# Moving two weight conversions from between the last token mixing products into the eighth and the last attention tile

## The chip, the cores and the metric

The kernel runs on one core of one Trainium2 chip. Its time is device microseconds from launch to end. TensorE (PE) multiplies, VectorE (DVE) and ScalarE (ACT) work on elements, GpSimd (POOL) takes some element work and the indirect transfers, SyncE (SP) issues nearly all other transfers.

## The reference, cut to what matters

Three blocks follow each other: an attention with a decaying state, a token and channel mixing block, and a mixture of experts whose expert is chosen token by token. All weights of the middle block are float64 in the input.

```python
def reference(r, k, v, w, u, moe_..., moe2_...):
    x = attention(r, k, v, w, u)            # 2 x 768 tokens x 384
    xt = x.transpose(0, 2, 1)
    h = np.maximum(xt @ w_tok1, 0.0) @ w_tok2      # token mixing, 768 -> 256 -> 768
    u = x + h.transpose(0, 2, 1)
    h2 = np.maximum(u @ w_ch1, 0.0) @ w_ch2        # channel mixing, 384 -> 1536 -> 384
    return moe2(u + h2, ...)                       # 8 experts, 384 -> 1024 -> 384
```

## The kernel before, in words

**Attention.** The 1536 tokens are 12 tiles of 128, and the loop `for t in range(NT)` makes one pass for each: passes 0 to 5 are the first batch, 6 to 11 the second. The instructions are written out by hand and every engine keeps its own order, so a late instruction holds back all that stand behind it on its engine. In pass t VectorE scales the inputs of tile t+2 (`pre_rk`, tile `rk`), masks the scores of tile t+1 (`masks`, two `am`), multiplies `pp` for tile t+2, and adds the output of tile t (`finish`, tile `x`). ScalarE then rounds `x` to `xh`, and GpSimd makes the remainder `xl` (L473); TensorE multiplies in pairs hi and lo.

**Conversions.** A float64 weight matrix arrives as pairs of 32-bit words in a buffer `raw` (two of them in turn, 768 KB each). There are 16 conversions, numbered 0 to 15, two halves for each of eight matrices: 0 and 1 for `t1`, 2 and 3 for `t2`, 4 and 5 for `c10`, 6 and 7 for `c20`, 8 and 9 for `c11`, 10 and 11 for `c21`, 12 and 13 for `c12`, 14 and 15 for `c22`. One conversion is

- ScalarE: an absolute value (L305, `conv_abs`);
- VectorE: two short operations (L314, L315) and two longer ones (L319, L321), in `conv_parts`; after the last one the load of the conversion two further on is issued (`conv_load`, L275);
- one step later (`conv_finish`): a rounding on ScalarE (L281) and a subtraction on GpSimd (L282) that gives the low part.

`CONV_T` lists the passes that hold conversions 0, 1, 2 and so on. `CONV_N` says how many of its steps stand ahead of `finish` in the pass. A pass without a conversion only finishes the one before it.

**Token mixing.** `mix1` runs in the passes and gathers into two accumulators. The second product (`mix2`) of the first batch has six parts: parts 1 to 5 stand in passes 7 to 11 and part 6 right behind the loop. All six use the same accumulator (`k=2`), and VectorE adds each part to `xT` (L515) before the next may start. In pass 10 `usplit(0)` lets VectorE make three `ul` tiles (L526) behind the addition of part 4.

**Behind the loop** stand `turn(11)`, the first two steps of channel mixing (`ch1` 0 and 1) with the last `mix1` between them, and the six parts of `mix2` for the second batch, which take three accumulators in turn. `conv_tail` puts conversions 8 and 9 between them, by `CONV_B` and `ABS_B`. From channel mixing's step 2 on, each step holds one more conversion, 10 to 15.

Of the kernel before, what the change touches and what calls it, by code (L numbers as in the profile page):

```python
# [28 lines left out]
W_LO, W_HI = 0.55, 1.25  # L29
WARM = (6, 12, 3)  # L30
T1 = 4
CONV_T = (2, 3, 4, 5, 6, 8, 9, 10)
CONV_B = (1, 1, 1, 1, 1, 1, 0, -1, 0, 0)
ABS_NEXT = (10, 11, 12, 13, 14)
ABS_B = (0, 3)
CONV_N = (0, 0, 0, 1, 1, 1, 1, 1, 1, 1, 1, 0)
HI_MIN, HI_MAX = (float(x) for x in np.array([0x38100000, 0x47EFFFFF], np.int32).view(np.float32))

# [33 lines left out]
@with_exitstack  # L72
def moe_chain_kernel(ctx, tc, a_in, wu, u_row, wt1, wt2, wc1, wc2, wgl, wex, cst_in, cst_a, out):
    with tc.manual_schedule():
        _emit(ctx, tc, a_in, wu, u_row, wt1, wt2, wc1, wc2, wgl, wex, cst_in, cst_a, out)


def _emit(ctx, tc, a_in, wu, u_row, wt1, wt2, wc1, wc2, wgl, wex, cst_in, cst_a, out):
# [55 lines left out]
    def load_a(t, part=None):  # L134
        if t not in a_t:
            rk = ap.tile([128, 1024], F32, tag="rk", name=f"rk{t}", bufs=4)
            v = ap.tile([128, DM], F32, tag="v", name=f"v{t}", bufs=3)
            a_t[t] = (rk, v)
        for p, (dst, c0) in enumerate(zip(a_t[t], (0, 1536))):
            if part is None or p == part:  # L140
                nc.sync.dma_start(out=dst, in_=a_in[t, :, c0:c0 + dst.shape[1]])
# [136 lines left out]
    def conv_finish():  # L278
        if conv_pend:
            f, hs, ls = conv_pend.pop()  # L280
            nc.scalar.copy(hs, f)  # L281
            nc.gpsimd.tensor_tensor(out=ls, in0=f, in1=hs.bitcast(F32), op=ALU.subtract)  # L282
# [4 lines left out]
    def conv_abs(n):  # L287
        k, h = conv[n]
        name = ("t1", "t2", "c10", "c20", "c11", "c21", "c12", "c22")[k]
        if h == 0:  # L290
            pool = wtp if k < 2 else wbl if k < 5 else wb2[0]
            W[name] = tuple(pool.tile([128, 1536], F32R, tag=f"b{2 * k + j}", name=name) for j in range(2))
        raw = conv_raw.pop(0)
        parts = tuple(x[:, h * 768:(h + 1) * 768] for x in W[name])
        if wb2:
            if n < 12:
                late[n % 2] = cpool_[0].tile([128, 1536], I32, tag=f"raw{6 + n % 2}", name="f")
            f, mag = late[n % 2][:, 0:768], late[n % 2][:, 768:1536].bitcast(F32)
        else:
            if n % 2:  # L300
                f = hp.tile([128, 768], I32, tag="row", name="f", bufs=1)
            else:
                f = ap.tile([128, 768], I32, tag="f", name="f", bufs=1)
            mag = f.bitcast(F32)
        nc.scalar.activation(out=mag, in_=raw[:, :, 1].bitcast(F32), func=ACTF.Abs)  # L305
        conv_mag[n] = raw, mag, f, parts

    def conv_parts():
# [16 lines left out]
                conv_abs(n + 1)  # L325
            yield
        conv_finish()

    tail_at = [-1]

    def conv_tail(n):
        tail_at[0] += 1
        for j in range(2):
            if ABS_B[j] == tail_at[0]:
                conv_abs(8 + j)
        if n < 0:
            conv_finish()
        else:
            conv_do(n)

    conv_work = conv_parts()

    def conv_do(n=3):
        for _ in range(n):
            next(conv_work, None)
# [68 lines left out]
    def values(t):  # L414
        b, c = divmod(t, NCH)
        rk, v = a_t[t]
        am = am_t.pop(t)
        y = ps_tile("y", (128, DM))
        for q in range(4):
            if c > 0:  # L420
                nc.tensor.matmul(y[:, q * 96:(q + 1) * 96], lhsT=rk[:, q * 128:(q + 1) * 128], rhs=sts[(t - 1) % 3][:, q], start=(q == 0), stop=False)
        for h in range(8):
            q, hh = divmod(h, 2)
            for g in range(2):
                r = slice(64 * g, 64 * g + 64)
                nc.tensor.matmul(y[r, h * D:(h + 1) * D], lhsT=am[hh][:, q, r], rhs=v[:, h * D:(h + 1) * D], start=(c == 0 and h == 0), stop=(h == 7))
        y_t[t] = y
# [27 lines left out]
    def state(t):  # L455
        kpv = kp_t[t]
        if t % NCH > 0:
            for q in range(4):
                nc.scalar.activation(out=sts[t % 3][:, q], in_=kpv[:, q], func=ACTF.Copy, scale=w128[:, q:q + 1])
            return  # L460
        for g in range(2):
            ps, cs = slice(64 * g, 64 * g + 64), slice(48 * g, 48 * g + 48)
            nc.vector.tensor_tensor(out=sts[t % 3][ps, :, cs], in0=kpv[ps, :, cs], in1=w128[ps].unsqueeze(2).to_broadcast([64, 4, 48]), op=ALU.mult)

    def finish(t):
        b, c = divmod(t, NCH)
        x = ap.tile([128, DM], F32, tag="x", name="x")
        nc.vector.tensor_tensor(out=x, in0=y_t.pop(t), in1=bon_t.pop(t).rearrange("p h e -> p (h e)"), op=ALU.add)
        nc.sync.dma_start(out=x, in_=yscr[t], cond=bad > 0, cond_hint=False)
        xh[t] = ap.tile([128, DM], F32R, tag=f"xh{c}", name=f"xh{t}", bufs=1)  # L470
        xl[t] = ap.tile([128, DM], F32R, tag=f"xl{c}", name=f"xl{t}", bufs=1)
        nc.scalar.copy(xh[t], x)
        nc.gpsimd.tensor_tensor(out=xl[t], in0=x, in1=xh[t].bitcast(F32), op=ALU.subtract)  # L473
        xx[t] = x

    def turn(t):
        b, c = divmod(t, NCH)
        if c == 0:
            xT[b] = xtp.tile([128, 3, S], F32, tag=f"xT{b}", name=f"xT{b}")
        x = xx.pop(t)  # L480
        tp = ps_tile("tp", (128, DM))
        for k in range(3):
            nc.tensor.transpose(tp[:, k * 128:(k + 1) * 128], x[:, k * 128:(k + 1) * 128], CA("ident"))
        nc.scalar.copy(xT[b][:, :, c * 128:(c + 1) * 128], tp.rearrange("p (k j) -> p k j", k=3))
# [6 lines left out]
    def mix1(t):  # L491
        b, c = divmod(t, NCH)
        w1h, w1l = W["t1"]
        if c == 0:
            mix_ps[b] = [acc_tile(m) for m in range(2)]
        for m in range(2):
            o = c * 256 + m * 128
            mm3(mix_ps[b][m], w1h[:, o:o + 128], w1l[:, o:o + 128], xh[t], xl[t], c == 0, c == NCH - 1)
        if c == NCH - 1:
            for m in range(2):  # L500
                hi = ap.tile([128, DM], F32R, tag=f"t1h{m}", name="t1h", bufs=1)
                lo = ap.tile([128, DM], F32R, tag=f"t1l{m}", name="t1l", bufs=1)
                relu_split(mix_ps[b][m], hi, lo)
                t1[m] = (hi, lo)

    def mix2(b, half, c, k=2):
        w2h, w2l = W["t2"]
        ps = acc_tile(k)
        for m in range(2):
            hi, lo = t1[m]  # L510
            o = m * S + half * 384
            cs = slice(c * 128, (c + 1) * 128)
            mm3(ps, hi[:, cs], lo[:, cs], w2h[:, o:o + 384], w2l[:, o:o + 384], m == 0, m == 1)
        u = xT[b][:, c, half * 384:(half + 1) * 384]
        nc.vector.tensor_tensor(out=u, in0=u, in1=ps, op=ALU.add)  # L515
# [37 lines left out]
    for t in range(NT):  # L553
# [16 lines left out]
        if grow:  # L570
            update(t + 1)
            state(t + 1)
        if t in CONV_T:
            conv_abs(CONV_T.index(t))
        values(t)
        if t + 1 < NT:
            pre_bonus2(t + 1)
        if t + 3 < NT:
            load_a(t + 3, 1)
        if t in CONV_T:  # L580
            conv_do(CONV_N[t])
        else:
            conv_finish()
        finish(t)
        if t in CONV_T:
            conv_do(3 - CONV_N[t])
# [73 lines left out]
    def chan_step(n, f, side, then):  # L660
        ps = ch1(f)
        if f >= 3:
            next(side, None)
        if f == 11:
            then()
        if f >= 3:
            next(side, None)
        h = hsplit(ps)
        push(lambda: ch2(n, f, h))
        if n == 3 and f == 11:  # L670
            unit_ready(0)
        work()

    def chan(n, side, then, start=0):
        for f in range(start, 12):
            chan_step(n, f, side, then)
        for _ in side:
            pass

    conv_tail(CONV_B[0])  # L680
    turn(11)
    chan_step(0, 0, nothing, None)
    conv_tail(CONV_B[1])
    mix1(11)
    conv_tail(CONV_B[2])
    chan_step(0, 1, nothing, None)
    conv_tail(CONV_B[3])
    for half in range(2):
        for c in range(3):
            mix2(1, half, c, (2, 0, 1)[c])  # L690
            conv_tail(CONV_B[4 + 3 * half + c])
    actx.close()

    wb2.append(ctx.enter_context(tc.tile_pool(name="wb2", bufs=1)))
# [657 lines left out]
```

## Time and profile before

| what | value |
|---|---|
| median of 3 runs | 432.24 us (431.27 to 433.52) |
| the profiled execution | 428.3 us, its span 426.8 us |
| TensorE busy | 407.2 us, 95% of the span |
| VectorE busy | 278.3 us, 65% |
| ScalarE busy | 192.7 us, 45% |
| GpSimd busy | 92.6 us, 22% |
| mean granted TensorE clock | 0.984 |

The span runs from the first to the last instruction; the profiled execution is one of the program, with the profiler on. Its time lies 3.9 us under the median, and the launch around the span takes 1.5 us of it.

### The profile page before, as it was taken

What the parts mean: (1) busy time and instruction counts of PE and PEld (TensorE: products, weight loads), DVE (VectorE), ACT (ScalarE), POOL (GpSimd) and SP (SyncE); (2) the same over time, 40 slices, a digit from 0 to 9 for tenths busy, and PEclk for the clock granted to TensorE, in tenths of its full rate; (3) what the DMA queues carried; (4) which work ended last, traced back from release to release, by engine and by line L of the source; (5) the groups of instructions that cost most, each with busy time, mean ns of one, the idle gap of its engine ahead of it and who ended that gap; (6) DMA issues with size and microseconds to landing.
All of it is one profiled execution on the core that took longest, in us unless ns stands there. A gap on an engine that the chain in (4) does not pass through costs nothing. (4 is left out here: it accounts for less than half of the span.)

```text
span 426.8 us, 8281 instructions
## 1 busy us (share of the span) xinstructions
PE 407.2 (95%) x3172; PEld 387.6 (91%) x3172; DVE 278.3 (65%) x590; ACT 192.7 (45%) x461; POOL 92.6 (22%) x83
## 2 busy tenths in 40 slices
PE   7999699998899799999999999999999999999994
PEld 4888598897798799999999999999999999999994
DVE  6859998788979944623362447568677677675431
ACT  2677468475443331213221221452755666655531
POOL 2014236236233310000000001131362132121110
PEclk9999999999999699999999999999999999999998
DMA  7544475132390000100100010871779866663000
GB/s 250 196 150 143 156 262 191 44 137 74 129 363 27 2 1 2 55 2 0 39 19 2 1 57 1 330 295 61 241 288 409 278 217 233 215 209 102 6 35 14
DMA packets 16799, 55.86 MB, mean 131 GB/s; under 512 B 3921, under 2 KB 7795, under 8 KB 16754
## 3 DMA queue, kind: packets, MB, share of 16 engines
q1 hardware_dynamic: 14834, 49.96, 33.3%
q0 software_dynamic: 1920, 5.32, 4.0%
q8 instruction: 26, 0.43, 0.4%
q14 instruction: 19, 0.16, 0.1%
HBM read 52.31 MB, written 5.91 MB: 136 GB/s over the span
## 5 line engine op out<-in xcount | busy, mean ns | idle before, releaser
L1014 DVE TENSOR_TENSOR we<-wr,we 128x768 fp32r<-128x768 f32 x54 | 51.6, 960 | 16.0 <-ACT we L1013 15.7
L353 ACT ACTIVATE hh<-c 128x384 fp32r<-128x384 f32 x48 | 23.5, 490 | 73.6 <-PE c L350 64.9
L354 DVE SCALAR_TENSOR_TENSOR hl<-c,hh 128x384 fp32r<-128x384 f32 x48 | 26.5, 553 | 42.9 <-ACT hh L353 42.9
L353 ACT ACTIVATE hh<-e 128x256 fp32r<-128x256 f32 (+1 forms) x72 | 25.2, 351 | 56.9 <-PE e L350 42.3
L348 PE MATMUL c<-uh,c 128*128 128x384 f32 x144 | 48.8, 339 | 2.1 <-ACT c L281 2.1
L348 PE MATMUL acc<-hh,c 128*128 128x384 f32 x144 | 50.2, 349 | 0.0
L354 DVE SCALAR_TENSOR_TENSOR hl<-e,hh 128x256 fp32r<-128x256 f32 (+1 forms) x72 | 27.2, 378 | 35.2 <-ACT hh L353 35.1
L349 PE MATMUL c<-uh,c 128*128 128x384 f32 x144 | 48.8, 339 | 1.2 <-POOL c L282 1.2
L349 PE MATMUL acc<-hh,c 128*128 128x384 f32 x144 | 48.8, 339 | 0.0
L350 PE MATMUL acc<-hl,c 128*128 128x384 f32 x144 | 48.8, 339 | 0.0
L350 PE MATMUL c<-ul,c 128*128 128x384 f32 x144 | 48.5, 337 | 0.0
L1013 ACT CAST we<-wr 128x768 fp32r<-128x768 f32 x56 | 46.1, 830 | 4.6 <-DMA wr<-in_wex 4.6
L348 PE MATMUL acc<-we,hh 128*128 128x384 f32 x120 | 42.6, 355 | 0.0
L349 PE MATMUL acc<-we,hl 128*128 128x384 f32 x120 | 40.3, 336 | 0.0
L350 PE MATMUL acc<-we,hh 128*128 128x384 f32 x120 | 40.2, 335 | 0.0
L282 POOL TENSOR_TENSOR c<-f,c 128x768 fp32r<-128x768 f32 x12 | 25.4, 2117 | 43.9 <-ACT c L281 43.9
L348 PEld LDWEIGHTS c<-uh,c 128*128 128x128 f32 x144 | 27.4, 190 | 2.4 <-ACT c L281 2.4
L349 PEld LDWEIGHTS c<-uh,c 128*128 128x128 f32 x144 | 27.4, 190 | 1.8 <-POOL c L282 1.8
L349 PEld LDWEIGHTS acc<-hh,c 128*128 128x128 f32 x144 | 27.5, 191 | 0.0
L350 PEld LDWEIGHTS acc<-hl,c 128*128 128x128 f32 x144 | 27.5, 191 | 0.0
L348 PEld LDWEIGHTS acc<-hh,c 128*128 128x128 f32 x144 | 27.5, 191 | 0.0
L350 PEld LDWEIGHTS c<-ul,c 128*128 128x128 f32 x144 | 27.3, 190 | 0.0
(227 smaller groups left out, 959.9 us busy)
## 6 DMA issues: line engine op xcount, KB each, us to landing
wr<-in_wex SPq DMA_DIRECT2D x32, 768.0 KB
raw<-in_wc SPq DMA_DIRECT2D x12, 768.0 KB
rk<-in_a_in SPq DMA_DIRECT2D x12, 512.0 KB
raw<-in_wt SPq DMA_DIRECT2D x4, 768.0 KB
v<-in_a_in SPq DMA_DIRECT2D x12, 192.0 KB
x<-yscr SPq DMA_DIRECT2D x12, 192.0 KB
xs<-rows SPq DMA_DIRECT2D x8, 192.0 KB
xs<-row SPq DMA_DIRECT2D x4, 192.0 KB
```

What stands on the lines that cost most here:

```text
L282: nc.gpsimd.tensor_tensor(out=ls, in0=f, in1=hs.bitcast(F32), op=ALU.subtract)
L348: nc.tensor.matmul(ps, lhsT=lh, rhs=rh, start=first, stop=False)
L349: nc.tensor.matmul(ps, lhsT=ll, rhs=rh, start=False, stop=False)
L350: nc.tensor.matmul(ps, lhsT=lh, rhs=rl, start=False, stop=last)
L353: nc.scalar.activation(out=hi, in_=ps, func=ACTF.Relu)
L354: nc.vector.scalar_tensor_tensor(out=lo, in0=ps, scalar=0.0, in1=hi.bitcast(F32), op0=ALU.max, op1=ALU.subtract)
L1013: nc.scalar.copy(hi[:, cs], raw[:, cs])
L1014: eng.tensor_tensor(out=lo[:, cs], in0=raw[:, cs], in1=hi[:, cs].bitcast(F32), op=ALU.subtract)
```

## The change: what it does

Conversion 5 goes from pass 8 to pass 7, and with it 6 from pass 9 to 8, 7 from 10 to 9. Conversion 8 goes from behind the loop into pass 10, conversion 9 into pass 11. `conv_tail` is gone; behind the loop one `conv_finish` is left, which rounds conversion 9 between `ch1` 0 and the last `mix1`. Nothing is added or taken out, apart from where things stand: the `raw` loads from number 7 to number 11 are issued one pass earlier with their conversions.

```diff
-CONV_T = (2, 3, 4, 5, 6, 8, 9, 10)
-CONV_B = (1, 1, 1, 1, 1, 1, 0, -1, 0, 0)
+CONV_T = (2, 3, 4, 5, 6, 7, 8, 9, 10, 11)
 ABS_NEXT = (10, 11, 12, 13, 14)
-ABS_B = (0, 3)
...
-    tail_at = [-1]
-
-    def conv_tail(n):
-        tail_at[0] += 1
-        for j in range(2):
-            if ABS_B[j] == tail_at[0]:
-                conv_abs(8 + j)
-        if n < 0:
-            conv_finish()
-        else:
-            conv_do(n)
...
-    conv_tail(CONV_B[0])
     turn(11)
     chan_step(0, 0, nothing, None)
-    conv_tail(CONV_B[1])
+    conv_finish()
     mix1(11)
-    conv_tail(CONV_B[2])
     chan_step(0, 1, nothing, None)
-    conv_tail(CONV_B[3])
     for half in range(2):
         for c in range(3):
             mix2(1, half, c, (2, 0, 1)[c])
-            conv_tail(CONV_B[4 + 3 * half + c])
     actx.close()
```

The lines that go make line numbers of the changed kernel smaller: by 2 in `conv_parts` (L314 becomes L312), by 14 from `mm3` to the attention loop (L515 becomes L501), by 18 at the end.

VectorE, from the addition of part 4 in pass 10 to that of part 6 behind the loop, before. `acc_1435`, `acc_1496` and `acc_1523` are parts 4, 5 and 6.

```order
L515 TENSOR_TENSOR xT_505<-xT_505,acc_1435 128x384
L526 TENSOR_TENSOR ul<-xT_505,uh 128x384 x3
L468 TENSOR_TENSOR x<-y,bon 128x384
L515 TENSOR_TENSOR xT_505<-xT_505,acc_1496 128x384
L515 TENSOR_TENSOR xT_505<-xT_505,acc_1523 128x384
L314 TENSOR_SCALAR f<-f 128x768
```

The same place now, where parts 4, 5 and 6 are `acc_1447`, `acc_1516` and `acc_1543`.

```order
L501 TENSOR_TENSOR xT_505<-xT_505,acc_1447 128x384
L512 TENSOR_TENSOR ul<-xT_505,uh 128x384 x3
L454 TENSOR_TENSOR x<-y,bon 128x384
L312 TENSOR_SCALAR f<-f 128x768
L313 TENSOR_SCALAR f<-f 128x768
L317 SCALAR_TENSOR_TENSOR f<-raw,f 128x768
L319 SCALAR_TENSOR_TENSOR f<-raw,f 128x768
L501 TENSOR_TENSOR xT_505<-xT_505,acc_1516 128x384
L501 TENSOR_TENSOR xT_505<-xT_505,acc_1543 128x384
```

The four operations of conversion 9 now stand between `x` of tile 11 and the addition of part 5.

GpSimd in passes 9 to 11 and just behind the loop, before: `xl_1341`, `xl_1428` and `xl_1493` belong to tiles 9, 10 and 11, and the subtractions between them to conversions 6 and 7.

```order
L282 TENSOR_TENSOR c_962<-f,c_961 128x768
L473 TENSOR_TENSOR xl_1341<-x,xh_1340 128x384
L282 TENSOR_TENSOR c_1298<-f,c_1297 128x768
L473 TENSOR_TENSOR xl_1428<-x,xh_1427 128x384
L282 TENSOR_TENSOR c_1298<-f,c_1297 128x768
L473 TENSOR_TENSOR xl_1493<-x,xh_1492 128x384
L600 MEMSET upb 128x256
```

The same place now, with `xl_1351`, `xl_1440` and `xl_1505` for tiles 9, 10 and 11.

```order
L280 TENSOR_TENSOR c_1197<-f,c_1196 128x768
L459 TENSOR_TENSOR xl_1351<-x,xh_1350 128x384
L280 TENSOR_TENSOR c_1197<-f,c_1196 128x768
L459 TENSOR_TENSOR xl_1440<-x,xh_1439 128x384
L459 TENSOR_TENSOR xl_1505<-x,xh_1504 128x384
L280 TENSOR_TENSOR c_1397<-f,c_1396 128x768
L586 MEMSET upb 128x256
```

The two subtractions in passes 9 and 10 now belong to conversions 6 and 7 at the rounding of those passes, none stands between tiles 10 and 11, and conversion 8's stands behind tile 11.

VectorE between `ch1` 0 and the second batch's first added part (`acc_1594`), before: `hl` are `ch1` 0 and 1, the two `t1l` belong to `mix1`.

```order
L354 SCALAR_TENSOR_TENSOR hl<-c_1542,hh 128x384
L319 SCALAR_TENSOR_TENSOR f<-raw,f 128x768
L354 SCALAR_TENSOR_TENSOR t1l<-acc_1135,t1h 128x384
L354 SCALAR_TENSOR_TENSOR t1l<-acc_1136,t1h 128x384
L321 SCALAR_TENSOR_TENSOR f<-raw,f 128x768
L354 SCALAR_TENSOR_TENSOR hl<-c_1574,hh 128x384
L314 TENSOR_SCALAR f<-f 128x768
L315 TENSOR_SCALAR f<-f 128x768
L515 TENSOR_TENSOR xT_1129<-xT_1129,acc_1594 128x384
L319 SCALAR_TENSOR_TENSOR f<-raw,f 128x768
L515 TENSOR_TENSOR xT_1129<-xT_1129,acc_1603 128x384
```

The same place now; the first added part is `acc_1600`.

```order
L340 SCALAR_TENSOR_TENSOR hl<-c_1556,hh 128x384
L340 SCALAR_TENSOR_TENSOR t1l<-acc_1143,t1h 128x384
L340 SCALAR_TENSOR_TENSOR t1l<-acc_1144,t1h 128x384
L340 SCALAR_TENSOR_TENSOR hl<-c_1586,hh 128x384
L501 TENSOR_TENSOR xT_1137<-xT_1137,acc_1600 128x384
L501 TENSOR_TENSOR xT_1137<-xT_1137,acc_1608 128x384
```

No conversion is left on VectorE in this stretch.

## Rows read from the trace of the kernel before

**Rows 1.** Stretches: length, busy PE, PEld, DVE, ACT, POOL; PE clock, DMA, GB/s.

```profile
82.39:90.56 8.17, 8.17 (x98) 7.01 (x97) 7.23 (x11) 5.18 (x17) 0.35 (x1) 1.00 0.30 98
...
97.21:103.95 6.74, 4.71 (x56) 4.20 (x55) 6.69 (x7) 2.60 (x6) 5.34 (x3) 1.00 0.34 117
...
109.62:118.02 8.40, 7.10 (x38) 6.10 (x38) 8.09 (x12) 2.85 (x4) 3.01 (x2) 1.00 0.41 107
```

**Rows 2.** Timeline of PE: start, us, instruction, idle before and its releaser.

```profile
94.68 0.44 PE L348 MATMUL acc<-t,t1h 128*128 128x384 f32 x1
...
99.23 0.44 PE L348 MATMUL acc<-t,t1h 128*128 128x384 f32 x1
...
103.95 0.44 PE L348 MATMUL acc<-t,t1h 128*128 128x384 f32 x1 [2.04 <-DVE xT L515]
...
115.54 0.44 PE L348 MATMUL acc<-t,t1h 128*128 128x384 f32 x1 [1.24 <-DVE xT L515]
...
118.02 0.34 PE L348 MATMUL c<-uh,c 128*128 128x384 f32 x1
...
121.14 0.33 PE L348 MATMUL c<-uh,c 128*128 128x384 f32 x1
```

**Rows 3.** Timeline of DVE, the end of pass 10 and pass 11.

```profile
97.84 5.13 DVE L526 TENSOR_TENSOR ul<-xT,uh 128x384 fp32r<-128x384 f32 x3
102.89 0.54 DVE L468 TENSOR_TENSOR x<-y,bon 128x384 f32<-128x384 f32 x1
```

**Rows 4.** Timeline of POOL, passes 10 and 11.

```profile
96.74 2.43 POOL L282 TENSOR_TENSOR c<-f,c 128x768 fp32r<-128x768 f32 x1 [2.79 <-ACT c L281]
99.12 1.33 POOL L473 TENSOR_TENSOR xl<-x,xh 128x384 fp32r<-128x384 f32 x1
100.41 2.14 POOL L282 TENSOR_TENSOR c<-f,c 128x768 fp32r<-128x768 f32 x1
```

**Rows 5.** Timeline of DVE, passes 3 and 4.

```profile
39.59 2.49 DVE L321 SCALAR_TENSOR_TENSOR f<-raw,f 128x768 int32<-128x768 int32 x1
42.00 2.04 DVE L363 TENSOR_TENSOR rk<-rk,PP 128x1024 f32<-128x1024 f32 x1
```

**Rows 6.** Timeline of POOL, passes 3 and 4.

```profile
38.80 2.46 POOL L282 TENSOR_TENSOR t<-f,t 128x768 fp32r<-128x768 f32 x1 [5.38 <-ACT t L281]
41.23 1.73 POOL L473 TENSOR_TENSOR xl<-x,xh 128x384 fp32r<-128x384 f32 x1
```

**Rows 7.** Timeline of DVE: x of pass 7, then pass 9.

```profile
71.18 0.55 DVE L468 TENSOR_TENSOR x<-y,bon 128x384 f32<-128x384 f32 x1
...
83.94 1.21 DVE L363 TENSOR_TENSOR rk<-rk,PP 128x1024 f32<-128x1024 f32 x1
85.08 1.27 DVE L409 TENSOR_TENSOR am<-at,cst 128x512 f32<-128x512 f32 x2
86.28 0.67 DVE L368 TENSOR_TENSOR pp<-rk 128x512 f32<-128x512 f32 x1
87.83 0.56 DVE L314 TENSOR_SCALAR f<-f 128x768 f32<-128x768 f32 x1 [0.87 <-ACT f L305]
88.42 0.56 DVE L315 TENSOR_SCALAR f<-f 128x768 int32<-128x768 int32 x1
88.90 0.55 DVE L468 TENSOR_TENSOR x<-y,bon 128x384 f32<-128x384 f32 x1
89.36 0.95 DVE L319 SCALAR_TENSOR_TENSOR f<-raw,f 128x768 int32<-128x768 int32 x1
90.35 0.96 DVE L321 SCALAR_TENSOR_TENSOR f<-raw,f 128x768 int32<-128x768 int32 x1
91.22 0.55 DVE L515 TENSOR_TENSOR xT<-xT,acc 128x384 f32<-128x384 f32 x1
```

**Rows 8.** Timeline of ACT, pass 10: the rounding of conversion 6.

```profile
95.84 0.82 ACT L281 CAST c<-f 128x768 fp32r<-128x768 f32 x1
```

**Rows 9.** Windows of PE alone: stretch, busy, PE clock, DMA share, GB/s.

```profile
102.00:103.00 1.00, 0.00 (x0) 1.00 0.00 0
142.15:147.04 4.89, 4.89 (x16) 0.51 0.02 5
```

**Rows 10.** Timeline of PE in channel mixing: step 8's two waits.

```profile
140.26 0.69 PE L348 MATMUL c<-uh,c 128*128 128x384 f32 x1 [2.11 <-ACT c L281]
142.15 0.69 PE L349 MATMUL c<-uh,c 128*128 128x384 f32 x1 [1.20 <-POOL c L282]
```

## The prediction

> **What bounds the kernel now.** TensorE is busy 95% of the span, so I read first the stretches in which it is not, then who it waits for. The table of stretches [rows 1] shows pass 9 full (8.17 of 8.17 us) and two holes near the change: pass 11 with part 6 still to come (4.71 of 6.74 us), and the six second-batch parts of the token mixing (7.10 of 8.40 us). TensorE's timeline [rows 2] names the waits. Part 6 starts at 103.95 after 2.04 us, released by VectorE's addition of part 5, since both use one accumulator. Between the second-batch parts the longest wait is 1.24 us at 115.54, for an addition that stands behind conversion 9 on VectorE. Later, step 8 of channel mixing waits 2.11 and 1.20 us [rows 10] for conversion 13.
>
> VectorE's and GpSimd's timelines say why VectorE is late in pass 11. Three `ul` take 5.13 us from 97.84, and `x` of tile 11 starts only at 102.89 [rows 3]; meanwhile GpSimd has three subtractions at 96.74, 99.12 and 100.41 [rows 4]. The two engines exclude each other, instruction by instruction, and take turns: passes 3 and 4 show it cleanly. L321 starts at 39.59 and ends at 42.08, 0.82 us behind GpSimd's subtraction, which ends at 41.26; the next on GpSimd, from 41.23, ends at 42.96, 0.88 us behind L321's end; `rk` ends at 44.04, 1.08 us behind that [rows 5, 6]. So a converting subtraction that found VectorE busy needs some 1.7 us of its own once VectorE lets go (from 39.59, where L321 stood ready, to 41.26), one of `xl` 0.88, and VectorE stands still for it. Operations that read PSUM (`am`, `x`, the additions of parts) I take as free of this.
>
> **Part 1: what the tail gets back.** Conversions 8 and 9 leave the stretch from 109.62 to 118.02. Its six parts are 36 multiplications. At the pace of step 2 of channel mixing, 18 in 3.12 us (118.02 to 121.14) [rows 2], they need 6.24 us. The stretch is 8.40 us [rows 1], so 2.16 us come back at most. I take it all: with VectorE free, the additions (0.55 us each) fit between three accumulators in turn. Step 2 and conversion 10 follow the end of the parts as before, so the later waits [rows 10] stay where they are, counted from step 2. **-2.16.**
>
> **Part 2: passes 7 to 10.** Pass 7 gets VectorE work that it had not. One pass with a conversion costs VectorE, start to start [rows 7], 0.59 (L314), 0.48 (L315), 0.46 (`x`), 0.99 (L319), 0.87 (L321), 0.46 (addition of a part), 1.14 (`rk`), 1.20 (two `am`) and 0.60 (`pp`), in all 6.8 us. GpSimd holds up L321 by about 1.5 us (1.7 less what overlaps) and `rk` by 0.4: 8.7 us. Conversion 5 can begin where `x` of pass 7 stood, at 71.18, so L314 comes at 71.2, 79.9 and 88.6 in passes 7, 8 and 9, and the addition of part 3 ends at 94.0. TensorE needs that for part 4 at 94.68 [rows 2], so nothing is lost yet: the cover is 0.7 us, and were it gone each microsecond would count in full. ScalarE's extra absolute value in pass 7 lies in its idle time. The moved `raw` loads and the input load queued behind one of them on SP's queue are issued some 8 us before their use, with the DMA engines 30% busy in pass 9 [rows 1]; I count zero for them too.
>
> **Part 3: passes 10 and 11.** Pass 10 has no `rk` and no `pp`: after two `am` its L314 stands at 95.2, then L315 95.8, `x` 96.2, L319 96.7. Conversion 7's rounding is done as conversion 6's is now, at about 96.6 [rows 8], and GpSimd gets in while `x` runs. Taking turns as in [rows 5, 6]:
>
> - GpSimd, conversion 7, to 98.4; L319 to 99.2; `xl` of tile 10 to 100.1; L321 to 100.9; addition of part 4 to 101.4. Part 5, now at 99.23 [rows 2], starts at 101.4.
> - three `ul` at 0.53 without a turn for GpSimd (nothing is ready there) to 102.9; `x` of tile 11 to 103.4.
> - conversion 9: L314 and L315 to 104.4; `xl` of tile 11 to 105.3; L319 to 106.1; conversion 8's subtraction to 107.85; L321 to 108.7; addition of part 5 to 109.1.
>
> Part 6 starts at 109.2 in place of 103.95 [rows 2]. **+5.2.** TensorE would stand still for 2.2 us ahead of part 5 and for 5.2 us ahead of part 6. Behind the waiting addition nothing else is late: `turn(11)`, `ch1` 0 and the last `mix1` follow part 6 in TensorE's own order, and conversion 9's rounding on ScalarE has 0.9 us that fit ahead of `t1h`.
>
> The bounds of this term: if GpSimd never held VectorE in pass 11, L321 would end at 106.3 and part 6 start at 106.8 (+2.8); if VectorE were not late into pass 10, `ul` would end with conversion 7 still to be served as now, `x` of tile 11 stand at 101.4 and part 6 at 107.8 (+3.85). Above, each further turn for GpSimd costs 0.9 or 1.7. I take 5.2, since every turn in it has its like in [rows 4] to [rows 6].
>
> By the Trainium skill, page "SBUF — State Buffer", section "SBUF: two separate sides", the port pair that both engines share is an exclusive lock, and whoever starts first has it for the whole instruction; it does not say that the one who waited goes next. If VectorE kept it from one instruction to the next in pass 11, the sum of terms so far would be +0.65 and not +3.1; the trace takes turns in rows 5 and 6, which is why I do not go by that.
>
> **Part 4: the clock.** A wait of 2.04 us ahead of part 6 left the granted clock at 1.00 (102 to 103). The waits of 2.11 and 1.20 us in channel mixing [rows 10] were followed by 0.51, the lower of the two levels (1.2 GHz), from 142.15 to 147.04: 16 multiplications took 4.89 us [rows 9], against 2.77 at 0.173 each, a loss of 2.1. The new holes, 2.2 and 5.2 us with 2.5 us of work between, are longer than that pair. I take **+2.0** once, for part 6 and what follows; the bounds are 0 (no fall) and 3.4, half of the 6.8 us from the slow multiplication at 140.26 [rows 10] to 147.04.
>
> By the Trainium skill, page "TensorE: Matmul & The Clock Gate", Part 1, the lower level is the default and activity lifts it. By it the fall is what to expect of a longer hole; by the row of 102 to 103 alone it would not come and the sum would be +3.1. No run here shows a single hole of 5 us.
>
> **Sum.** -2.16 + 5.2 + 2.0 = +5.1 us: 433.4 for the profiled execution of 428.3, whose span is 426.8. That execution lies 3.9 us under the median, so on the median of 432.24 I forecast 437.3 us, 1.2% slower. Half a percent, 2.16 us, is about what a measurement of this kernel can tell from no change.
>
> **The rivals.**
>
> - *The clock holds.* All as above without the 2.0: 435.3. For it: the 2.04 us wait cost no clock. Against it: the new holes are longer. Chance 0.17.
> - *VectorE is less late.* It keeps up in passes 7 to 10, or GpSimd does not get its turns in pass 11. Then terms 1 to 3 give +0.65 (5.2 replaced by 2.8) to +1.7 (by 3.85), and with the clock's 2.0 up to +3.7: 432.9 to 435.9. For it: VectorE idles 0.87 us ahead of L314 in pass 9 [rows 7], so it catches up when it can. Against: 8.7 us a pass against TensorE's 8.17. Chance 0.16, half of it within half a percent.
> - *The other side: conversion 9 ends in time.* Without a third GpSimd subtraction behind `xl` of tile 10, `ul` could be done by 99.5 if VectorE came into pass 10 as early as now and GpSimd were through; then `x` of tile 11 at 99.5, four operations of 2.9 us, and the addition of part 5 by 103.4, no later than today's 103.9. Part 6 stays, the tail's 2.16 are kept: 430.1, or 430.0 to 431 if a little is lost. It decides at the start of `x` of tile 11: before 100.0 there is no loss ahead of part 6, and each later microsecond costs one. Against: that needs all 3.4 us of GpSimd's turns gone. Chance 0.07, mostly at the edge of half a percent.
> - *The change does not do what it says*: the second-batch parts keep their waits for another reason, or hole and gain cancel, 431 to 434. Chance 0.10.
>
> My forecast has 0.50. Faster by over 0.5%: the larger part of the third rival with a little noise, 0.07. Within 0.5%: half of the second rival, 0.08, the fourth, 0.09, a little of the third, 0.01: 0.18. Slower: the rest, 0.75. The range for 8 in 10 goes from 432.9, the low end of the second rival, to 438.7, where the clock costs 3.4 (432.24 + 3.1 + 3.4); some 0.12 lies below, the rest above.
>
> **What the profile of the changed kernel would show.** Part 1 is right if the six second-batch parts take 6.2 to 6.5 us from start to end and no wait for an addition is left between them. Part 2: no TensorE wait in passes 7 to 9, and L314 of conversion 6 some 8.7 us behind that of conversion 5. Part 3: a TensorE wait near 2.2 us ahead of part 5 and one near 5 us ahead of part 6, both for L501; L317 or L319 of conversion 9 lasting over 1.5 us with GpSimd's subtraction beside it. Part 4: a granted clock near 0.5 in the microseconds around part 6 and `ch1` 0. The forecast falls if `x` of tile 11 starts before 101, if L317 and L319 there take 0.95 us each, or if the wait ahead of part 6 is as short as today's.

## The result, and the profile after

The changed kernel takes 435.62 us (median of 10 runs, 433.6 to 441.06) against 432.25 us for the kernel before (median of 10 runs in the same job): ratio 1.009, 95% interval 1.0065 to 1.0116. That is 3.9 us slower (0.009 x 432.25; 2.8 to 5.0 by the interval). A few executions of either kernel are 1 to 2% longer (up to 440.43 and 441.06 us); the medians hold them, the ratio leaves them out. The forecast was slower, 437.3 us, with 432.9 to 438.7 as its range.

The profiled execution took 434.85 us, its span is 433.2 us and its mean granted clock 0.977, where before had 426.8 us and 0.984. So the two profiles differ by 6.4 us, more than the timed runs do. The first question is therefore which part of the 6.4 us belongs to the change. I read TensorE's timeline at fixed points of the program: the scores of pass 7, parts 5 and 6, the first second-batch part and step 2 of channel mixing. One row of before that was not shown yet gives its start of pass 7:

```profile
65.16 1.16 PE L397 MATMUL at<-rk 64*128 64x128 f32 x16
```

The same points of the changed kernel (start, us, instruction, idle before and its releaser), answering to [rows 2]:

```profile
66.71 1.16 PE L383 MATMUL at<-rk 64*128 64x128 f32 x16
...
102.79 0.45 PE L334 MATMUL acc<-t,t1h 128*128 128x384 f32 x1 [1.94 <-DVE xT L501]
...
110.39 0.69 PE L334 MATMUL acc<-t,t1h 128*128 128x384 f32 x1 [4.90 <-DVE xT L501]
...
118.65 0.34 PE L334 MATMUL acc<-t,t1h 128*128 128x384 f32 x1
...
125.00 0.33 PE L334 MATMUL c<-uh,c 128*128 128x384 f32 x1
```

Subtracting gives the account. Pass 7 starts 1.55 us later (66.71 less 65.16), ahead of the first thing that the change moves. From there to part 6 it takes 43.68 us instead of 38.79: +4.89. From part 6 to the first second-batch part it takes 8.26 us instead of 5.67: +2.59. The second-batch parts take 6.35 us instead of 8.40: -2.05. From pass 7 to step 2 that makes +5.43; the remainder up to the end of the span takes 308.20 us instead of 308.78. 1.55 + 5.43 - 0.58 is the 6.4 us. Below, the six second-batch parts are also called the tail.

The list of TensorE's waits (what, for whom, us in total, times, longest) says the same in its first line; before, L515 stood there with the waits of [rows 2].

```profile
PE acc L334 <- DVE xT L501: 6.8, 2, 4.9
```

Stretches of the changed kernel (length, busy PE, PEld, DVE, ACT, POOL, PE clock, DMA, GB/s), answering to [rows 1]: from part 5 to part 6, and the second-batch parts.

```profile
102.80:110.40 7.60, 2.70 (x16) 2.34 (x16) 7.43 (x9) 1.82 (x4) 4.29 (x4) 0.92 0.33 103
118.65:125.00 6.35, 6.35 (x37) 6.35 (x37) 3.53 (x7) 0.49 (x1) 0.69 (x1) 1.00 0.01 3
```

In the first row VectorE is busy for 7.43 of 7.60 us and TensorE for 2.70: the hole is VectorE's. In the second TensorE has no gap at all. (A VectorE instruction that is held up counts as busy; the rows below show how much of the 7.43 us that is.) VectorE's timeline shows the pace of the passes (the L312 rows) and what fills the hole:

```profile
72.71 0.55 DVE L312 TENSOR_SCALAR f<-f 128x768 f32<-128x768 f32 x1
...
81.36 0.55 DVE L312 TENSOR_SCALAR f<-f 128x768 f32<-128x768 f32 x1
...
89.97 0.55 DVE L312 TENSOR_SCALAR f<-f 128x768 f32<-128x768 f32 x1
...
102.19 0.54 DVE L501 TENSOR_TENSOR xT<-xT,acc 128x384 f32<-128x384 f32 x1
102.66 1.48 DVE L512 TENSOR_TENSOR ul<-xT,uh 128x384 fp32r<-128x384 f32 x3
104.06 0.54 DVE L454 TENSOR_TENSOR x<-y,bon 128x384 f32<-128x384 f32 x1
...
105.70 1.63 DVE L317 SCALAR_TENSOR_TENSOR f<-raw,f 128x768 int32<-128x768 int32 x1
107.37 2.49 DVE L319 SCALAR_TENSOR_TENSOR f<-raw,f 128x768 int32<-128x768 int32 x1
109.79 0.54 DVE L501 TENSOR_TENSOR xT<-xT,acc 128x384 f32<-128x384 f32 x1
```

GpSimd in that hole:

```profile
105.37 1.15 POOL L459 TENSOR_TENSOR xl<-x,xh 128x384 fp32r<-128x384 f32 x1 [3.92 <-ACT xh L458]
106.48 2.57 POOL L280 TENSOR_TENSOR c<-f,c 128x768 fp32r<-128x768 f32 x1
```

Read the two together: `xl` ends at 106.52 and L317 at 107.33; GpSimd's conversion 8 then ends at 109.05, 1.72 us later, and L319 at 109.86, 0.81 us behind that. Both engines are held up in turn, as in [rows 5, 6]; only then can the addition of part 5 start at 109.79 and part 6 at 110.39.

The clock, in windows of PE alone (length, busy, granted clock, DMA share, GB/s):

```profile
108.00:109.00 1.00, 0.00 (x0) 1.00 0.00 0
109.00:110.00 1.00, 0.00 (x0) 0.60 0.00 0
110.00:111.00 1.00, 0.61 (x2) 0.50 0.42 49
...
115.00:116.00 1.00, 1.00 (x5) 0.50 0.60 220
116.00:117.00 1.00, 1.00 (x7) 0.99 0.00 0
```

It falls to 0.50, the lower level (1.2 GHz), while TensorE stands still ahead of part 6, and stays there until 116.0. The same instructions, from part 6 to the last `mix1`, take 5.60 us here (110.39 to 115.99) and 3.05 us before (103.95 to 107.00); that is nearly all of the 2.59 us above.

### The profile page after: what moved, and what is told of

Same layout as the page of the kernel before. It is cut to its first block, busy times and chain, and to the rows that moved or that the text cites. A ratio compares the mean times of both kernels' runs of the same rounds, so it can differ in the third digit from the quotient of the medians.

```text
span 433.2 us, 8281 instructions
## 1 busy us (share of the span) xinstructions
PE 409.8 (95%) x3172; PEld 391.3 (90%) x3172; DVE 282.5 (65%) x590; ACT 192.1 (44%) x461; POOL 92.8 (21%) x83
## 5 line engine op out<-in xcount | busy, mean ns | idle before, releaser
L280 POOL TENSOR_TENSOR c<-f,c 128x768 fp32r<-128x768 f32 x12 | 23.6, 1963 | 51.7 <-ACT c L279 49.6
L335 PEld LDWEIGHTS acc<-hh,c 128*128 128x128 f32 x144 | 27.3, 190 | 0.0
L334 PE MATMUL e<-gx,we 128*128 128x256 f32 x96 | 27.3, 284 | 0.0
```

The lines of the kernel that those rows point to most:

```text
L334: nc.tensor.matmul(ps, lhsT=lh, rhs=rh, start=first, stop=False)
L335: nc.tensor.matmul(ps, lhsT=ll, rhs=rh, start=False, stop=False)
```

## The experiments

The column "pass 7 to step 2" is read from each profile at the two points used above. It leaves out what differs ahead of pass 7 and, in the medians, from run to run. Each ratio is against the kernel before on the same chip; before's median there is 432.16 us for e_part_first to e_late_low, 430.61 us for e_eight_last to e_best and 431.93 us for e_combo, so go by the ratios and not by the medians.

| run | what is different | ratio (95%) | median us | span us | pass 7 to step 2, us |
|---|---|---|---|---|---|
| before, first profile | | 1 | 432.25 | 426.8 | 52.86 |
| e_before_again | nothing | one run | 432.53 | 430.9 | 54.42 |
| after | the change | 1.009 (1.0065 to 1.0116) | 435.62 | 433.2 | 58.29 |
| e_part_first | after, part 5's addition ahead of conversion 9 | 0.9948 (0.9922 to 0.9974) | 429.83 | 426.6 | 51.73 |
| e_nine_back | only conversions 5 to 8 early | 0.9977 (0.9949 to 1.0006) | 430.16 | 427.6 | 52.71 |
| e_fill | after, TensorE kept busy | 1.0039 (1.0004 to 1.0075) | 433.25 | 431.7 | 56.01 |
| e_late_low | after, one GpSimd turn later | 1.0017 (0.9988 to 1.0046) | 432.81 | | |
| e_eight_last | conversion 8 in pass 11, no lateness | 1.0102 (1.0051 to 1.0153) | 435.31 | 434.4 | 58.01 |
| e_five_early | only conversions 5 to 7 early | 0.9948 (0.9912 to 0.9985) | 427.9 | 426.3 | 50.55 |
| e_best | after, additions of parts 4 and 5 first | 1.0022 (0.9998 to 1.0047) | 431.68 | 428.9 | 53.37 |
| e_combo | conversions 5 to 8 early, additions first | 0.9875 (0.9824 to 0.9925) | 426.43 | 424.7 | 49.18 |

The profile of e_late_low has a lower mean clock than all others (0.953), so only single instructions and VectorE's pace are read from it.

### e_part_first: is it the order on VectorE?

After, with the addition of part 5 ahead of conversion 9 in pass 11. All the work stays.

```diff
-        if t in CONV_T:
+        if t in CONV_T and t != 11:
             conv_do(3 - CONV_N[t])
         if t >= 7:
             mix2(*m2.pop(0))
+        if t == 11:
+            conv_do(3)
```

> The changed kernel, with one exchange in pass 11: the addition of part 5 stands ahead of conversion 9 on VectorE instead of behind it. My theory (the loss is conversion 9 standing ahead of the addition that part 6 waits for): the wait ahead of part 6, 4.9 us in the changed kernel, goes to under 0.5 us, the granted clock stays at 1.00 there, the wait of 1.9 us ahead of part 5 stays, and the time falls by some 6 us against the changed kernel, to 1 to 2 us under the kernel before (ratio to before 0.995 to 0.998). Rival (VectorE's lateness out of passes 7 to 10 is the loss, the order in pass 11 only shows it): the wait ahead of part 6 stays over 3 us and the ratio to before stays over 1.004.

Measured: 0.9948, where after has 1.009. TensorE's two waits in this stretch are now

```profile
102.69 0.44 PE L334 MATMUL acc<-t,t1h 128*128 128x384 f32 x1 [1.88 <-DVE xT L501]
...
111.58 0.44 PE L334 MATMUL acc<-t,t1h 128*128 128x384 f32 x1 [0.63 <-ACT t1h L339]
```

The wait ahead of part 5 is as in after; that ahead of part 6 is gone, and 0.63 us came up ahead of the second-batch parts. Pass 7 to step 2 shrinks by 6.56 us: 4.90 of the wait and 2.59 of the clock, less 0.63 and some 0.3 in smaller gaps. One exchange of two groups of instructions removes the loss, so the loss was the place of conversion 9 ahead of the addition, not its work.

### e_nine_back: conversion 9 back between the second-batch parts

Before, with conversions 5 to 8 one step early and 9 where it was.

```diff
-CONV_T = (2, 3, 4, 5, 6, 8, 9, 10)
-CONV_B = (1, 1, 1, 1, 1, 1, 0, -1, 0, 0)
+CONV_T = (2, 3, 4, 5, 6, 7, 8, 9, 10)
+CONV_B = (0, 0, 0, 1, 1, 1, 0, -1, 0, 0)
-ABS_B = (0, 3)
+ABS_B = (99, 3)
```

> Half of the change: conversions 5 to 8 stand one pass earlier as in the changed kernel, conversion 9 stays between the second-batch parts where the kernel before has it. My theory: part 5 waits some 2 us as in the changed kernel, part 6 waits 0 to 1.5 us, no fall of the clock there, and the second-batch parts take 6.3 to 7 us, so the ratio to before is 0.996 to 1.001. Rival (lateness out of passes 7 to 10 is the loss): a wait over 3 us ahead of part 6 remains and the ratio is 1.005 or more. Rival (the tail's waits are conversion 9's alone): the six second-batch parts still take over 8 us.

Measured: 0.9977, not to be told from no change. The wait ahead of part 5 remains:

```profile
102.72 0.69 PE L348 MATMUL acc<-t,t1h 128*128 128x384 f32 x1 [1.89 <-DVE xT L515]
```

Part 6 has no wait left (it starts at 106.76), and the second-batch parts take 7.0 us (112.40 to 119.40). So with conversion 9 still in it the tail gives back 1.4 of its 2.05 us. VectorE's L319 of conversion 9 runs undisturbed there:

```profile
115.44 0.95 DVE L319 SCALAR_TENSOR_TENSOR f<-raw,f 128x768 int32<-128x768 int32 x1
```

In before, conversion 8's GpSimd subtraction stands beside L319, which takes 2.16 us and ends 0.81 us behind the subtraction (115.01 and 114.20); e_eight_last, below, has the same.

```profile
112.85 2.16 DVE L319 SCALAR_TENSOR_TENSOR f<-raw,f 128x768 int32<-128x768 int32 x1
```

```profile
111.92 2.28 POOL L282 TENSOR_TENSOR c<-f,c 128x768 fp32r<-128x768 f32 x1 [6.09 <-ACT c L281]
```

The first multiplication of part 5 lasts 0.69 and not 0.44: in this profile the wait of 1.89 us was followed by the lower clock (0.50 in 103 to 106).

### e_fill: what is the clock's share?

After, with 24 multiplications of a constant tile into an accumulator of their own in the hole ahead of part 6. Nothing of the computation changes, and TensorE's wait for the addition is covered rather than removed.

```diff
+    fill = ps_tile("fill", (128, 384))
+    for _ in range(24):
+        nc.tensor.matmul(fill, lhsT=warm[:, 0:128], rhs=warm[:, 0:384], start=True, stop=True)
     nc.gpsimd.memset(upb[:, 128:384], 1.0)
```

> The changed kernel, with 24 multiplications of zeros into a spare PSUM bank between the last mix1 of pass 11 and part 6, so that TensorE works through about 4 us of the 4.9 us hole (nothing of the computation changes). My theory, part 4: the granted clock stays at 1.00 through part 6 and channel mixing's first steps, part 6 still starts about 4.9 us behind the end of mix1, and the time falls by 1.7 to 2.3 us against the changed kernel (ratio to before 1.003 to 1.006). Rival (the lower clock is hidden, since VectorE or ScalarE sets the pace there anyway): the same time as the changed kernel, ratio 1.009.

Measured: 1.0039 against 1.009, some 2.2 us (0.0051 x 432). The windows at part 5 and from part 6 on:

```profile
103.64:107.90 4.26, 4.26 (x16) 0.60 0.60 185
111.51:115.00 3.49, 3.49 (x23) 1.00 0.91 292
```

Part 6 now runs at 1.00. In this profile, though, the clock fell at the shorter wait ahead of part 5 (1.91 us), which after's profile (1.94 us) does not show; the added work began later for it, and part 6 starts 7.87 us behind part 5 instead of 7.60. The two intervals overlap (up to 1.0075 here, from 1.0065 there), so 2.2 us is a rough size; from pass 7 to step 2 the two profiles differ by 2.28 us, and the count for after above is 2.59.

### e_late_low: one GpSimd turn out of the hole

After, with conversion 8's rounding and its subtraction on GpSimd behind `turn(11)`.

```diff
+        if t == 11:
+            held = conv_pend.pop()
...
     turn(11)
+    nine = conv_pend.pop()
+    conv_pend.append(held)
+    conv_finish()
+    conv_pend.append(nine)
     chan_step(0, 0, nothing, None)
```

> The changed kernel, with conversion 8's rounding and GpSimd subtraction put behind turn(11), out of the hole; the amount of work is the same. If taking turns with GpSimd's subtraction is part of the hole as I worked it out: L319 of conversion 9 (2.5 us in the changed kernel) takes about 0.95 us, L317 stays near 1.6 us beside xl of tile 11, the wait ahead of part 6 falls from 4.9 to some 3.3 us, and the time by 1.5 us (ratio to before 1.003 to 1.007, and lower if the clock does not fall). Rival (the two engines do not hold each other up, the long L319 has another cause): it still takes about 2.5 us, wait and time as in the changed kernel.

Measured: 1.0017, under the 1.003 to 1.007 that was expected if the clock still falls. VectorE's two longer operations of conversion 9:

```profile
114.34 1.65 DVE L317 SCALAR_TENSOR_TENSOR f<-raw,f 128x768 int32<-128x768 int32 x1
116.03 0.96 DVE L319 SCALAR_TENSOR_TENSOR f<-raw,f 128x768 int32<-128x768 int32 x1
```

and TensorE's waits:

```profile
111.43 0.69 PE L334 MATMUL acc<-t,t1h 128*128 128x384 f32 x1 [1.91 <-DVE xT L501]
...
117.50 0.44 PE L334 MATMUL acc<-t,t1h 128*128 128x384 f32 x1 [1.85 <-DVE xT L501]
```

L319 went from 2.49 to 0.96: GpSimd's turn cost VectorE 1.53 us, and part 6 starts 6.07 us behind part 5 instead of 7.60, the same 1.53. The wait itself fell by more (4.90 to 1.85) because TensorE ran at the lower clock between the two parts here (0.50 in 112 to 114) and was itself late. The time fell by some 3.2 us (0.0073 x 432), more than the 1.53. That the rest is a smaller loss of clock is not shown: in this profile the clock falls behind part 6 as well (0.50 in 119 to 121).

### e_before_again: how steady is the profile of before?

The kernel before, unchanged, profiled once more.

> The kernel before, profiled once more, unchanged. In the profiles of the changed kernel and of the experiments, pass 7 starts 1.5 us or more later than in the one of before, though the order of all engines is the same up to there. If this is how long the clock happens to stay at its lower level in passes 4 and 5, this profile can show either start of pass 7 (65.2 or 66.7); if the change does it, pass 7 starts at 65.2 again.

Measured: 432.53 us. Pass 7 starts at 67.55 in this profile, 65.16 in the first. So the 1.55 us that after is late there is within what the unchanged program shows. The same wait ahead of part 6 as in [rows 2] was this time followed by a fall of the clock:

```profile
106.34 0.45 PE L348 MATMUL acc<-t,t1h 128*128 128x384 f32 x1 [2.03 <-DVE xT L515]
```

```profile
107.00:108.00 1.00, 1.00 (x5) 0.50 0.00 0
108.00:109.00 1.00, 1.00 (x6) 0.50 0.00 2
```

Pass 7 to step 2 took 54.42 us, 1.56 more than in the first profile. Against this profile the change costs 3.87 us, against the first 5.43.

### e_eight_last: pass 11 alone

Before, with conversion 8 in pass 11 ahead of the addition of part 5; 5 to 7 stay as before, and so does 9. VectorE comes into pass 10 as early as before.

```diff
-CONV_T = (2, 3, 4, 5, 6, 8, 9, 10)
+CONV_T = (2, 3, 4, 5, 6, 8, 9, 10, 11)
```

(`CONV_B` and `ABS_B` as in e_nine_back.)

> Conversions 5 to 7 stand where the kernel before has them, conversion 8 stands in pass 11 ahead of the addition of part 5, conversion 9 stays between the second-batch parts. So pass 11 holds four operations of a conversion without any lateness out of passes 7 to 9. My theory: part 5 does not wait, part 6 waits 5 to 6 us for the addition of part 5, the second-batch parts take some 7 us, and the ratio to before is 1.004 to 1.011. Rival (lateness out of passes 7 to 9 makes the loss): part 6 waits under 3 us and the ratio is under 1.002.

Measured: 1.0102, as slow as the whole change.

```profile
109.91 0.69 PE L348 MATMUL acc<-t,t1h 128*128 128x384 f32 x1 [5.59 <-DVE xT L515]
...
123.07 0.44 PE L348 MATMUL acc<-t,t1h 128*128 128x384 f32 x1 [1.23 <-DVE xT L515]
```

A conversion ahead of that addition makes TensorE wait whether or not the passes ahead hold more work. On before's time base (pass 7 starts 2.40 us later here) part 6 stands at 107.51, +3.56 against before, where the prediction's bound for a VectorE that is not late had 107.8. The rest of the 5.15 us that the column shows over before is the clock, which is at 0.50 from 109 to 113: from part 6 to the first second-batch part 7.44 us (109.91 to 117.35) in place of 5.67, less 0.18 us in the tail.

The tail keeps its wait with one conversion in it (8.22 us, 117.35 to 125.57), where e_nine_back had none. VectorE's and GpSimd's rows show the difference:

```profile
120.39 2.16 DVE L319 SCALAR_TENSOR_TENSOR f<-raw,f 128x768 int32<-128x768 int32 x1
```

```profile
119.63 2.11 POOL L282 TENSOR_TENSOR c<-f,c 128x768 fp32r<-128x768 f32 x1 [10.44 <-ACT c L281]
```

L319 ends at 122.55, 0.81 us behind GpSimd's 121.74, and takes 1.21 us more than in e_nine_back. The 1.23 us wait of the tail is thus a turn of GpSimd too, conversion 8's, and not the amount of VectorE's work.

### e_five_early: passes 7 to 9 alone

Before, with only conversions 5 to 7 one pass early; 8 and 9 stay in the tail.

```diff
-CONV_T = (2, 3, 4, 5, 6, 8, 9, 10)
+CONV_T = (2, 3, 4, 5, 6, 7, 8, 9)
```

> The other half: conversions 5, 6 and 7 one pass earlier as in the changed kernel, conversions 8 and 9 where the kernel before has them, so passes 10 and 11 hold none. My theory (moving into pass 7 costs nothing, the order in passes 10 and 11 does): no TensorE wait for VectorE in passes 7 to 11, part 6 waits under 0.5 us, the second-batch parts take 8.4 us as before, and the ratio to before is 0.993 to 0.998. Rival (lateness out of pass 7 costs): a wait ahead of part 4 or 5 of over 1 us and a ratio of 0.999 or more.

Measured: 0.9948. The only wait for an addition that is left is the 1.23 us one in the tail:

```profile
114.77 0.44 PE L348 MATMUL acc<-t,t1h 128*128 128x384 f32 x1 [1.23 <-DVE xT L515]
```

VectorE's timeline in passes 10 and 11, answering to [rows 3]:

```profile
98.16 3.03 DVE L526 TENSOR_TENSOR ul<-xT,uh 128x384 fp32r<-128x384 f32 x3
101.12 0.54 DVE L468 TENSOR_TENSOR x<-y,bon 128x384 f32<-128x384 f32 x1
```

`ul` takes 3.03 us instead of 5.13, since conversion 6's subtraction on GpSimd is done a pass earlier, so that two stand there and not three:

```profile
97.20 1.84 POOL L282 TENSOR_TENSOR c<-f,c 128x768 fp32r<-128x768 f32 x1 [1.38 <-ACT c L281]
99.00 1.31 POOL L473 TENSOR_TENSOR xl<-x,xh 128x384 fp32r<-128x384 f32 x1
```

Pass 10 also holds no conversion on VectorE here, so `ul` starts 1.22 us earlier (98.16 less the 1.54 us by which pass 7 starts later, against 97.84). `x` of tile 11 ends in time for part 6. This half of the change is a gain, of 2.31 us by the column.

### e_best: additions first in passes 10 and 11

After, with the additions of parts 4 and 5 ahead of what is left of conversions 8 and 9, and `ul` split off behind the addition of part 5.

```diff
-        if t in CONV_T:
+        if t in CONV_T and t < 10:
             conv_do(3 - CONV_N[t])
...
         if t == 10:
-            usplit(0)
+            usplit(0, (True, False))
+        if t == 11:
+            usplit(0, (False, True))
+        if t >= 10:
+            conv_do(3 - CONV_N[t])
```

> The changed kernel with three exchanges on VectorE: the additions of parts 4 and 5 stand ahead of what is left of conversions 8 and 9 in passes 10 and 11, and the three ul come behind the addition of part 5. My theory: neither part 5 nor part 6 waits over 0.5 us, the second-batch parts take 6.3 to 7 us, and the ratio to before is 0.987 to 0.994, under that of the kernel with only part 5's addition moved (0.995). Rival (VectorE has no more room, each exchange only moves the wait on): the waits ahead of part 6, of ch1 0 or of the first second-batch part grow to 1.5 us or more together and the ratio stays 0.994 to 0.997.

Measured: 1.0022, a miss: above the range of the theory and above that of the rival. The waits ahead of parts 5 and 6 are gone and a new one has come, ahead of the first second-batch part:

```profile
111.91 0.69 PE L334 MATMUL acc<-t,t1h 128*128 128x384 f32 x1 [2.96 <-ACT t1h L339]
```

ScalarE's timeline says why:

```profile
110.63 0.83 ACT L279 CAST c<-f 128x768 fp32r<-128x768 f32 x1 [3.78 <-DVE f L319]
111.37 0.86 ACT L339 ACTIVATE t1h<-acc 128x384 fp32r<-128x384 f32 x2
```

`t1h` stands behind the rounding of conversion 9, which waits for L319. The conversion that no longer held the addition held ScalarE instead. On VectorE it was late for a new reason as well:

```profile
105.20 2.82 DVE L312 TENSOR_SCALAR f<-f 128x768 f32<-128x768 f32 x1
```

L312, 0.55 us elsewhere, ends at 108.02, behind GpSimd's subtraction (until 107.00) and two clearing operations that write only (until 107.60).

### e_combo: what the runs point to

Conversion 9 stays in the tail (as in e_nine_back), the additions of parts 4 and 5 come first (as in e_best), and conversion 8's rounding and GpSimd subtraction go behind `xh` of tile 11.

`CONV_T` is as in e_nine_back, `CONV_B` and `ABS_B` too, and `usplit` takes its second argument as in e_best.

```diff
...
-        else:
+        elif t < 11:
             conv_finish()
         finish(t)
-        if t in CONV_T:
+        if t in CONV_T and t < 10:
             conv_do(3 - CONV_N[t])
...
         if t == 10:
-            usplit(0)
+            usplit(0, (True, False))
+            conv_do(3 - CONV_N[t])
+        if t == 11:
+            usplit(0, (False, True))
+            conv_finish()
```

> What the runs so far point to: conversions 5 to 8 one pass earlier as in the changed kernel, conversion 9 between the second-batch parts as before; on VectorE the additions of parts 4 and 5 ahead of what is left of conversion 8, and the three ul behind the addition of part 5; conversion 8's rounding behind xh of tile 11. My theory (only what stands ahead of an addition that TensorE waits for costs): parts 5 and 6 and the first second-batch part wait under 0.3 us each, the six second-batch parts take some 7.0 us, and the ratio to before is 0.988 to 0.994. Rival (VectorE is full there, and the wait moves to the tail as in the kernel with three exchanges): waits of 1.5 us or more between mix1 and step 2 and a ratio of 0.996 or more.

Measured: 0.9875 (0.9824 to 0.9925), 426.43 us: faster than both kernels. Parts 5 and 6 start without a wait:

```profile
101.34 0.44 PE L348 MATMUL acc<-t,t1h 128*128 128x384 f32 x1
...
103.86 0.34 PE L348 MATMUL acc<-t,t1h 128*128 128x384 f32 x1
```

and from part 5 to step 2 TensorE has no idle time that the timeline lists. Pass 7 to step 2 is 3.68 us shorter than in before's first profile.

## Why the prediction was right

**What bounds the kernel.** TensorE, held by VectorE's additions through the one accumulator. Confirmed: the two long waits of after are of that kind, and e_part_first takes the larger away by order alone.

**Part 1, the tail: -2.16, measured -2.05.** The tail takes 6.35 us in place of the 6.24 forecast, and no wait is listed in it. The prediction put the tail's 1.24 us wait down to the addition's place behind conversion 9; the runs show that 1.2 of it is conversion 8's GpSimd subtraction beside L319 (e_nine_back against e_eight_last).

**Part 2, passes 7 to 9 at nothing.** Right in after: no TensorE wait in them, and L312 of conversion 6 stands 8.65 us behind that of conversion 5 (forecast 8.7). What the prediction did not price is that the earlier place of conversions 5 to 7 is by itself a gain: it takes a GpSimd subtraction away from `ul`, and a conversion away from VectorE ahead of it, and so the 2.04 us of [rows 2] (e_five_early). Its second rival set VectorE's 8.7 us a pass against TensorE's 8.17; that is pass 9, while passes 7 and 8 take TensorE 8.61 and 8.62 us in before, so VectorE hardly falls behind in them. In the whole change the wait that conversions 8 and 9 make covers it.

**Part 3, passes 10 and 11: +5.2, measured +4.89.** Both waits came where they were forecast: 1.94 for 2.2 ahead of part 5, 4.90 for 5.2 ahead of part 6. With the 1.55 us of late start taken off, part 6 stands at 108.84 for 109.2. The turns of the two engines came in the forecast order, 1.63 us for L317 and 2.49 for L319. By the Trainium skill, page "SBUF — State Buffer", section "SBUF: two separate sides", the shared pair of ports is an exclusive lock for a whole instruction; the trace agrees: L319 ends 0.81 us behind GpSimd's 109.05, with 0.95 of its own. The prediction's variant in which VectorE goes on from one instruction to the next without a turn for GpSimd (+0.65) did not occur.

The bound of this part for a VectorE that comes into pass 10 on time was part 6 at 107.8 (+3.85); e_eight_last, which comes nearest to that case, has 107.51 (+3.56). The price of GpSimd's turns was "0.9 or 1.7" each; taking one away (e_late_low) gave 1.53.

**Part 4, the clock: +2.0, measured 2.59 in the profile.** The lower level came where it was forecast, and e_fill shows that keeping TensorE busy there is worth some 2.2 us.

**The sum.** +5.1 forecast (the terms as printed add up to 5.04), +5.43 from pass 7 to step 2 in the two first profiles, +3.9 in the timed runs. The term that may be too large for the timed runs is the clock's, and for a reason that the prediction had not thought of: it took before's 2.04 us wait as free of clock loss, from one profile. In the second profile of before the same wait cost 1.56 us, and against that one the change costs 3.87. Where before's timed runs lose the clock can't be seen, as they have no trace, but their mean clock is listed. Of the 68 beside the experiments 4 have the 0.984 of the first profile, and these took 428.3 to 428.4 us as it did; the others have 0.983 or less. So the first profile is before at its fastest. That the loss ahead of part 6 explains all of the 1.2 us is argued, not shown.

The prediction also carried before's 3.9 us between the profiled execution and the median over to the changed kernel. There the distance is 0.8 us (434.85 and 435.62). It had the profiled execution 1.5 us too low (433.4; pass 7 started 1.55 us late) and that distance 3.1 us too large; that the two errors partly cancel in the 437.3 is luck. The terms of the change itself are not: each came within 0.6 us of its forecast in the two first profiles.

**The rivals.** *The clock holds* gave 435.3, close to the measured 435.6, but its mechanism did not happen in the profile: the clock fell. The range of *VectorE is less late* reaches 435.9, so the time alone does not decide against it either; the rows do. It and *conversion 9 ends in time* fail on `x` of tile 11, which starts at 104.06 (102.5 on before's time base, where the limits were 101 and 100.0), and on L317 and L319. *The change does not do what it says* fails on the tail.

## What to carry to other kernels

When work moves into an earlier stage to fill an idle engine, look at which instruction of that engine the bounding engine waits for next, and put that one ahead of the moved work: here the same change costs 0.9% with conversion 9 ahead of one addition and gains 0.5% with it behind. Then follow the moved work's successors on the other engines in their order, since a wait that is taken off one queue may come up on the next (`t1h` on ScalarE in e_best). And move only as much as pays: conversions 5 to 7 alone gained 0.5%, and one conversion ahead of part 5's addition, without them, lost 1%.

## What the runs showed of the hardware that was not expected

- The clock's loss after the same short wait differs between profiles of one program: ahead of part 6 of before, 2.04 us of wait left 1.00 in one profile, 2.03 us left 0.50 in the next. Waits of 1.9 us ahead of part 5 were followed by full clock in after and e_part_first and by the lower one in e_fill and e_nine_back.
- The start of pass 7 moved by 2.4 us (65.16 and 67.55) between two profiles of the unchanged kernel. In the first the clock was back at 1.00 by 56 us, in the second it was at 0.50 for all of 50 to 58. The same window, first of the first profile and then of the second:

```profile
56.00:58.00 2.00, 2.00 (x15) 1.00 0.52 191
```

```profile
56.00:58.00 2.00, 2.00 (x9) 0.50 0.58 189
```

- A short one-input VectorE operation was held up too: L312 took 2.82 us in e_best, until 0.42 us behind two GpSimd operations that only write, and in e_part_first L313 took 1.26 us in place of 0.56, until 0.41 us behind `xl`.
